# Attention score bursts of 9 and 10 banks, and P tiles that take the place expected to be free first

## The chip, the cores and the metric

One core of a Trainium2 chip. The metric is device time in microseconds (us). TensorE (PE; its weight loads are PEld), VectorE (DVE), ScalarE (ACT), GpSimd (POOL) and SyncE (SP) each run their own instructions in order and wait for one another by semaphores; DMAs are issued from the queues of SP, ACT and POOL.

## The reference, cut to what matters

The output is a mix of two branches over the same input of 2048 tokens by 1024. The change touches only the attention branch: 32 heads of 32 columns each.

```python
qkv = (x @ wqkv).reshape(B, S, 3, H, Dh).transpose(2, 0, 3, 1, 4)
q, k, v = qkv[0], qkv[1], qkv[2]
scores = jnp.einsum("bhqd,bhkd->bhqk", q, k) * (Dh ** -0.5)
p = _softmax(scores, axis=-1)
o = jnp.einsum("bhqk,bhkd->bhqd", p, v)
a = o.transpose(0, 2, 1, 3).reshape(B, S, D) @ wo
...
return g * a + (1 - g) * b
```

S is 2048, H is 32, Dh is 32; everything is float32. The other branch (b, a choice among 64 experts) and the gate g are worked out ahead of the attention's heads and behind them.

## The kernel before, in words

The program runs in three stages. From the start to about 628 us it makes q, k and v, the expert branch and the sums for the last products. From there to about 1650 us it works off the 32 heads, one behind the other: this is the stage of the change. Behind it come the products with wo and the output.

A head has 16 key tiles of 128 keys (kt, 0 to 15). For one tile, TensorE makes scores of 128 keys against 2048 queries: four matmuls of 512 queries, each into one of the banks of a ring of 7 PSUM banks (L1305, tile `ring`). Each matmul has a weight load of its own. ScalarE takes 1 to 4 neighbouring banks of the ring at a time, and writes exp of them into a P tile of 128 by 2048 in SBUF (L1319). A bank may be written again once its exp has ended. TensorE then multiplies P with V, 32 columns for each of four quarters of the queries side by side (L1330), and sums over the 16 tiles in one PSUM bank, `o`; behind the last tile ScalarE copies it out (`finish`, L1429, tile `osb`).

The row sums of P are made beside this: VectorE adds the tiles of a head into `acc`, two instructions a tile (L1366). Three tiles of each head (kt 3, 8 and 12, the rest of the list SUMS at L1340) are added by a DMA from POOL's queue into `accd` instead (L1354), and kt 1 is written straight into `accd`. When a head is over, VectorE adds `acc` and `accd` (merge), and further DMAs and adds fold the sums of up to four heads into one tile, of which `head_sums` makes the row sums by a matmul (L1345) into one bank of the ring.

A P tile lives in one of 11 places in SBUF (P0 to P7, and the tiles named vhl, wo_raw2 and wo_raw3, which serve for weights near the end). In the last third there are 9 and then 8 places. `p_tile` hands them out in rotation. A place can be written again when P·V and the add, or the DMA, that read its old tile have ended; ScalarE waits for that ahead of a tile's first exp.

The order of the work is written out by the loop at L1550 to L1565. It counts half tiles: `ends` gives where each burst of scores ends, 4 half tiles (8 banks) or 5 (10 banks), seven bursts a head, of 8, 8, 8, 10, 10, 10 and 10 banks. A half tile is 256 of each 512 queries, so that two banks make one half of a tile; two of a head's bursts end in the middle of a tile. Behind each burst stands P·V up to four half tiles behind the last score, then what `todo` has for these tiles (finish, merges, folds, loads for the next head on SP's queue), and the tile's add (`presum`). `scores` (L1282) sets by `cuts` where one exp ends and the next begins: at the burst's end, at a tile's end, at the ring's end, and behind the first bank, or the first three in a burst of 10.

Of the kernel before, what the change touches and what calls it, by code (L numbers as in the profile page):

```python
# [13 lines left out]
AF = mybir.ActivationFunctionType  # L14
# [5 lines left out]
H = 32  # L20
KC = D // 128
HC = KC // 2
NT = S // 128
NQ = S // 512
G = H // 4
W = 256
SCALE = 32 ** -0.5
# [5 lines left out]
def gated_mha_peer_kernel(ctx, tc, xT, wqkv, wv, wo, wq, k12, ug, v, out):  # L33
# [8 lines left out]
    nc = tc.nc  # L42
# [301 lines left out]
    places = {(2, 0): "xh2", (2, 1): "xl1", (3, 0): "xh3", (3, 1): "xl2"}  # L344
# [361 lines left out]
    for blk, (k, n) in enumerate(order):  # L706
        w, c = chunks[k]
        t = pairs[k % 2]
# [441 lines left out]
    P, pools, keep = {}, {}, None  # L1150


    RING = (11, 0), (9, 28 * 11), (8, 28 * 11 + 12 * 9)
    LATE = 21, 28

    def p_tile(h, kt):


        k, (n, i) = pools["next"], RING[0]
        for places, i0 in RING[1:]:  # L1160
            if k >= i0:
                n, i = places, i0
        i = (k - i) % n
        pools["next"] += 1
        pool, name = ((pools["right"], f"P{i}") if i < 4 else (pools["left"], f"P{i}") if i < 8 else
                      (keep, ("vhl", "wo_raw2", "wo_raw3")[i - 8]))
        P[h, kt] = pool.tile([128, S], F32, name=name)
        return P[h, kt]

    def first_scores():  # L1170

        tp.close()
        pools.update(right=Pool("ppr", side="right"), next=0)
        K, Q = Z
        pt = p_tile(0, 0)
        for qc, i in enumerate((5, 6, 0, 1)):
            ps = ps1.tile([128, 512], F32, name=f"bk{i}")
            c = slice(qc * 512, (qc + 1) * 512)
            nc.tensor.matmul(ps, K[:98, :128], Q[:98, c], start=True, stop=True)
            nc.scalar.activation(pt[:, c], ps, AF.Exp, scale=SCALE)  # L1180
# [48 lines left out]
    NB = 7  # L1229
    ring = pss.tile([128, NB, 512], F32, name="ring")  # L1230
# [30 lines left out]
    nc.vector.memset(KQ[1][0][96:98, :].bitcast(F32), 1.0)  # L1261
    load_head(1)

    def by_half(t):

        return t.rearrange("p (q f m) -> p q f m", q=NQ, f=2)

    def parts_of(u0, u1):

        while u0 < u1:  # L1270
            (h, u), whole = divmod(u0, 2 * NT), u0 % 2 == 0 and u0 + 1 < u1
            yield h, u // 2, None if whole else u % 2
            u0 += 2 if whole else 1

    def columns(t, part, i, m=1):

        f = part[2]
        if f is None:
            return t[:, i * 512:(i + m) * 512].rearrange("p (a m) -> p a m", a=m)
        return by_half(t)[:, 2 * i:2 * (i + m), f, :]  # L1280

    def scores(u0, u1):  # L1282


        of = [(part, i) for part in parts_of(u0, u1) for i in range(NQ if part[2] is None else 2)]
        n = len(of)
        banks = ring_banks(n)
        ends = {c for c in range(1, n + 1) if c == n or of[c][1] == 0 or banks[c] == 0}
        if n > 2 * NQ:
            cuts = ends | {1, 2, 3}  # L1290
        else:
            cuts = ends | {1}
            cuts |= {c + 2 for c in range(NQ, n, NQ) if not cuts & {c + 1, c + 3}}
        c0 = 0
        for c, i in enumerate(banks):
            part, j = of[c]
            h, kt, f = part
            K, Q = KQ[h % 2]
            if f is None:
                q = Q[:98, j * 512:(j + 1) * 512]  # L1300
                s = ring[:, i, :]
            else:
                q = by_half(Q)[:98, 2 * j:2 * j + 2, f, :]
                s = ring[:, i, :].rearrange("p (a m) -> p a m", a=2)
            on_ring(nc.tensor.matmul(s, K[:98, kt * 128:(kt + 1) * 128], q, start=True, stop=True), i)  # L1305
            if c + 1 not in cuts:
                continue
            m = c + 1 - c0
            j -= m - 1
            if j == 0 and f != 1:  # L1310
                if kt == SUMS[h == H - 1][0]:
                    P[h, kt] = ACCD[h] = wk.tile([128, S], F32, name="accd")
                else:
                    p_tile(h, kt)
            i -= m - 1
            s = ring[:, i:i + m, :]
            if f is not None:
                s = s.rearrange("p a (b m) -> p (a b) m", b=2)
            on_ring(nc.scalar.activation(columns(P[h, kt], part, j, m), s, AF.Exp, scale=SCALE),  # L1319
                    *range(i, i + m))  # L1320
            c0 = c + 1

    def pv(h, kt, f):
        g, j = divmod(h, 4)
        p = P[h, kt]
        if kt == 0 and f != 1:
            O[h] = pso.tile([128, 512], F32, name="o")
        c0, c1 = (0, 512) if f is None else (256 * f, 256 * f + 256)
        for qc in range(NQ):
            nc.tensor.matmul(O[h][32 * qc:32 * qc + 32, c0:c1], Vt[g][:, kt, 32 * j:32 * j + 32],  # L1330
                             p[:, qc * 512 + c0:qc * 512 + c1], start=(kt == 0), stop=(kt == NT - 1))
# [4 lines left out]

    SUMS = (1, 3, 8, 12), (2, 4, 6)  # L1340

    def rowsum(ps, *srcs, ones=ones):
        for src in srcs:
# [5 lines left out]
    def presum(h, kt):  # L1349
        sums = SUMS[h == H - 1]  # L1350
        if kt == 0 or kt == sums[0] or (h == H - 1 and kt >= NT - 2):
            return
        if kt in sums:
            nc.gpsimd.dma_start(ACCD[h], P[h, kt], accum_op=OP.add)  # L1354
            return
        if kt == 1 + (sums[0] == 1):
            if h > 0:
                ACC[h] = wk.tile([128, S], F32, name="acc")
            add(ACC[h], P[h, 0], P[h, kt])
        else:  # L1360
            add(ACC[h], ACC[h], P[h, kt])
# [185 lines left out]
    at((H - 1) * NT + 2, load_rb, 0, 0, KC - 1, range(2, 4))  # L1547


    LAG, LAST = 4, 2 * NT * H  # L1550
    ends = [6] + [2 * NT * h + e for h in range(H - 1) for e in (8, 12, 16, 21, 26, 31, 36)]
    ends += [*range(ends[-1] + 4, LAST + 1, 4), LAST + LAG]
    u0, v0, k = 2, 0, 0
    for u1 in ends:
        scores(u0, min(u1, LAST))
        v1 = 2 if u1 == 6 else u1 - LAG
        for part in parts_of(v0, v1):
            pv(*part)
        while 2 * k + 2 <= u1:
            for f, a in todo.pop(k, []):  # L1560
                f(*a)
            if k < NT * H:
                presum(*divmod(k, NT))
            k += 1
        u0, v0 = u1, v1  # L1565
    assert not todo
    pss.close()
    pools["left"].close()
# [281 lines left out]
```

## Time and profile before

| | us |
|---|---|
| three runs: median (lowest, highest) | 1819.63 (1819.18, 1826.15) |
| the execution that was profiled: its own time | 1828.57 |
| its span, from the first to the last instruction | 1826.8 |
| PE busy in it | 1813.0 |
| DVE busy | 1499.7 |
| ACT busy | 1229.4 |
| exps into the places named P (L1319, 917 instructions) | 735.9 |

The profile shows one execution. A line of the order in time has the start, the time from the start of the first to the end of the last of the instructions that it merges, the engine, the line of the program, the operation, out and in, and a count; in brackets is how long the engine had been idle ahead of it and who ended that. PE counts as busy while a matmul is in its pipeline, so waits on TensorE are seen better in the distances between its weight loads. Windows give the busy time of each engine in a stretch, and behind them the granted clock of TensorE, the mean busy share of the 16 DMA engines and GB/s.

### The profile page before, as it was taken

How to read it: one execution, taken by the hardware profiler on the slowest of the kernel's cores; microseconds unless marked ns; L12 is line 12 of the kernel's file. 1: busy time of each engine (PE TensorE's matmuls, PEld its weight loads, DVE VectorE, ACT ScalarE, POOL GpSimd, SP SyncE). 2: the span in 40 equal slices, each digit the busy share in tenths (PEclk: the TensorE clock that was granted, in tenths of full speed). 3: DMA queues.
4: the chain of work that ended last, by engine and by line, in shares of the span. 5: the costliest groups of instructions: out<-in, count | busy, mean ns of one | idle time of the engine just before them, and what ended most of it. 6: DMA issues, size and time to landing. Idle time of an engine off the chain costs nothing.

```text
span 1826.8 us, 27633 instructions
## 1 busy us (share of the span) xinstructions
PE 1813.0 (99%) x10383; PEld 1130.7 (62%) x10383; DVE 1499.7 (82%) x1673; ACT 1229.4 (67%) x1618; POOL 261.5 (14%) x314
## 2 busy tenths in 40 slices
PE   9999999999999999999999999999999999999999
PEld 7777777788888744445444444454444444447887
DVE  7868785368987788998989999898999898996674
ACT  4434422211243499999999999999899999993221
POOL 0222000036301211111111111111111011101000
PEclk9999999999999999999999999999999999999999
DMA  6788888722248689999999999999999998976861
GB/s 234 238 281 257 266 264 308 254 65 98 81 150 288 220 187 198 193 184 200 179 200 197 196 212 196 191 195 205 186 194 204 190 205 185 199 171 206 278 171 58
DMA packets 132224, 364.72 MB, mean 200 GB/s; under 512 B 17540, under 2 KB 57876, under 8 KB 106168
## 3 DMA queue, kind: packets, MB, share of 16 engines
q0 software_dynamic: 22064, 136.07, 37.8%
q1 hardware_dynamic: 89864, 190.94, 35.0%
q10 hardware_dynamic: 20160, 35.92, 7.0%
q8 instruction: 82, 1.34, 0.3%
q14 instruction: 54, 0.44, 0.1%
HBM read 169.14 MB, written 72.10 MB: 132 GB/s over the span
## 4 chain that ended last, share of the span: by engine, by line
PE 87%; DMA 10%; ACT 1%; DVE 1%; issue 0%; POOL 0%; SPq 0%; ACTq 0%; DVEq 0%; POOLq 0%
PE ring L1305 23%; PE o L1330 21%; PE bk L157 12%; PE bk L713 10%; DMA accd<-P 6%; PE pa L157 6%; PE bk L760 5%; PE pa L1594 2%; PE bk L928 2%; DMA accd<-wo_raw 2%; PE bk L313 2%; PE bk L493 1%; PE pa L1601 1%; PE bk L397 1%; DMA wraw<-in_wqkv 1%; ACT P L1319 1%
## 5 line engine op out<-in xcount | busy, mean ns | idle before, releaser
L1319 ACT ACTIVATE P<-ring 128x512 f32<-128x512 f32 (+3 forms) x917 | 735.9, 903 | 19.7 <-DMA accd<-P 5.2
L1366 DVE TENSOR_TENSOR acc<-acc,P 128x1024 f32<-128x1024 f32 x512 | 586.9, 1216 | 5.8 <-ACT P L1319 5.5
L1330 PE MATMUL o<-P,V 128*32 128x512 f32 (+1 forms) x3464 | 373.1, 551 | 0.0
L1305 PE MATMUL ring<-Q,K 98*128 98x512 f32 x1024 | 275.9, 410 | 3.2 <-ACT P L1319 2.2
L1305 PE MATMUL ring<-z,z 98*128 98x512 f32 x1020 | 275.9, 411 | 2.0 <-ACT P L1319 1.9
L1305 PEld LDWEIGHTS ring<-Q,K 98*128 98x128 f32 x1024 | 183.5, 188 | 133.8 <-ACT P L1319 44.4
L1305 PEld LDWEIGHTS ring<-z,z 98*128 98x128 f32 x1020 | 182.7, 188 | 132.0 <-ACT P L1319 43.8
L1330 PEld LDWEIGHTS o<-P,V 128*32 128x32 f32 x3464 | 94.7, 109 | 185.5 <-issue 167.8
L1354 POOL DMA_DIRECT2D accd<-P x76 | 69.2, 910 | 469.4 <-ACT P L1319 277.2
L1366 DVE TENSOR_TENSOR rb<-acc,accd 32x1024 f32<-32x1024 f32 (+2 forms) x60 | 70.7, 1217 | 52.1 <-DMA accd<-P 38.9
L1319 ACT ACTIVATE wo_raw<-ring 128x512 f32<-128x512 f32 (+2 forms) x135 | 110.1, 899 | 3.3 <-DMA accd<-wo_raw 1.5
L242 ACT ACTIVATE hi<-bk 128x512 fp32r<-128x512 f32 x40 | 23.7, 595 | 112.4 <-PE bk L713 93.2
L713 PE MATMUL bk<-xh,e 128*128 128x512 f32 x384 | 94.2, 394 | 0.0
L713 PE MATMUL bk<-xl,e 128*128 128x512 f32 x384 | 92.2, 389 | 0.0
L1366 DVE TENSOR_TENSOR acc<-acc,wo_raw 128x1024 f32<-128x1024 f32 x74 | 86.0, 1216 | 0.1
L713 PEld LDWEIGHTS bk<-xh,e 128*128 128x128 f32 x384 | 71.0, 188 | 22.0 <-issue 3.4
L713 PEld LDWEIGHTS bk<-xl,e 128*128 128x128 f32 x384 | 72.1, 188 | 15.0
L1319 ACT ACTIVATE vhl<-ring 128x512 f32<-128x512 f32 (+3 forms) x97 | 80.7, 900 | 0.9 <-PE ring L1305 0.2
L255 DVE TENSOR_TENSOR lo<-bk,hi 128x512 fp32r<-128x512 f32 x40 | 27.6, 689 | 65.1 <-ACT hi L242 62.7
L103 DVE TENSOR_TENSOR e<-wraw,e 128x512 fp32r<-128x512 f32 (+3 forms) x64 | 54.9, 867 | 29.7 <-ACT e L102 28.9
L102 ACT ACTIVATE e<-wraw 128x512 fp32r<-128x512 f32 (+3 forms) x64 | 44.7, 705 | 41.5 <-DMA wraw<-in_wqkv 26.1
L157 PE MATMUL bk<-xh,e 128*128 128x512 f32 x288 | 68.7, 393 | 0.0
(305 smaller groups left out, 2539.4 us busy)
## 6 DMA issues: line engine op xcount, KB each, us to landing
accd<-P POOLq DMA_DIRECT2D x76, 1024.0 KB, 11.6
wqt<-in_wq SPq DMA_DIRECT2D x26, 1024.0 KB
wraw<-in_wqkv SPq DMA_DIRECT2D x30, 512.0 KB
accd<-wo_raw POOLq DMA_DIRECT2D x11, 1024.0 KB, 12.5
rb<-acc POOLq DMA_DIRECT2D x36, 256.0 KB, 7.7
qdh<-hi ACTq DMA_DIRECT2D x32, 256.0 KB
qdl<-lo ACTq DMA_DIRECT2D x32, 256.0 KB
kdh<-hi ACTq DMA_DIRECT2D x32, 256.0 KB
```

The costliest lines, as they stand in the source:

```text
L102: nc.scalar.activation(hi, src, AF.Copy)
L103: (on or nc.vector).tensor_tensor(out=lo, in0=src, in1=hi.bitcast(F32), op=OP.subtract)
L157: nc.tensor.matmul(ps, self.a[a][i][:, k, :], self.b[b][j][k], start=(not first and k == 0 and i == j == 0), stop=(k == HC - 1 and i == 1))
L313: nc.tensor.matmul(ps[32 * quad:32 * quad + 32, :], kpad[:, quad % 2, i, :], t[:, quad, :], start=(i == 0), stop=(i == 3))
L713: nc.tensor.matmul(ps, t[:, kc // HC, a, kc % HC], x_at(b, n, kc), start=first, stop=last)
L760: nc.tensor.matmul(ps, x_at(a, t // 4, kc)[:, tok], b, start=first, stop=last)
L928: nc.tensor.matmul(p, x_at(a, t // 4, kc)[:, tok], b, start=first, stop=last)
L1305: on_ring(nc.tensor.matmul(s, K[:98, kt * 128:(kt + 1) * 128], q, start=True, stop=True), i)
L1319: on_ring(nc.scalar.activation(columns(P[h, kt], part, j, m), s, AF.Exp, scale=SCALE), *range(i, i + m))
L1330: nc.tensor.matmul(O[h][32 * qc:32 * qc + 32, c0:c1], Vt[g][:, kt, 32 * j:32 * j + 32], p[:, qc * 512 + c0:qc * 512 + c1], start=(kt == 0) ...
L1354: nc.gpsimd.dma_start(ACCD[h], P[h, kt], accum_op=OP.add)
L1366: nc.vector.tensor_add(out[:, c], a[:, c], b[:, c])
```

## The change

The loop counts banks, not half tiles. A head's bursts have 9, 9, 9, 10, 9, 9 and 9 banks (in the order in which they lie from a head's start: the first of them, up to the end at 73, ends 9 banks into the next head), and may end behind any bank of a tile. Scores of a bank are always of 512 neighbouring queries; the half tiles of 256 remain for P·V alone, which follows 8 banks behind, rounded down to a half tile. The first exps of one bank are now one in a burst of 8, two in a burst of 9, three in a burst of 10. In the last head the bursts have 8 banks as before.

`p_tile` keeps for each place the tile number at which it is expected to be free (`until`): 14 tiles on for a tile that a DMA adds, 4 for any other. It takes the place with the smallest number.

```diff
-        k, (n, i) = pools["next"], RING[0]
-        for places, i0 in RING[1:]:
-            if k >= i0:
-                n, i = places, i0
-        i = (k - i) % n
+        n = [places for places, k in PLACES if pools["next"] >= k][-1]
         pools["next"] += 1
+        i = min(range(n), key=lambda i: until[i])
+        until[i] = h * NT + kt + (14 if kt in SUMS[h == H - 1] else 4)
...
-        of = [(part, i) for part in parts_of(u0, u1) for i in range(NQ if part[2] is None else 2)]
-        n = len(of)
+        n = s1 - s0
         banks = ring_banks(n)
-        ends = {c for c in range(1, n + 1) if c == n or of[c][1] == 0 or banks[c] == 0}
-        if n > 2 * NQ:
-            cuts = ends | {1, 2, 3}
-        else:
-            cuts = ends | {1}
+        cuts = {c for c in range(1, n + 1) if c == n or (s0 + c) % NQ == 0 or banks[c] == 0}
+        cuts |= set(range(1, max(1, n - NB) + 1))
+        if n <= 2 * NQ:
             cuts |= {c + 2 for c in range(NQ, n, NQ) if not cuts & {c + 1, c + 3}}
...
-    LAG, LAST = 4, 2 * NT * H
-    ends = [6] + [2 * NT * h + e for h in range(H - 1) for e in (8, 12, 16, 21, 26, 31, 36)]
-    ends += [*range(ends[-1] + 4, LAST + 1, 4), LAST + LAG]
+    LAG, HEAD = 2 * NQ, NQ * NT
+    ends = [3 * NQ] + [HEAD * h + e for h in range(H - 1) for e in (18, 27, 36, 46, 55, 64, 73)]
+    ends[-1] -= 1
+    ends += [*range(ends[-1] + LAG, HEAD * H + 1, LAG), HEAD * H + LAG]
...
-        v1 = 2 if u1 == 6 else u1 - LAG
+        v1 = 2 if s1 == 3 * NQ else (s1 - LAG) // 2
```

On TensorE, at the turn from head 0 to head 1 (Q_5228 and K_5227 are head 1's, z_ are head 0's; a P·V row of 32x512 is a whole tile, one of 32x256 a half), the order before is:

```order
L1305 MATMUL ring<-z_4627,z_4626 128x512 x10
L1330 MATMUL o<-wo_raw_5371,V 32x512 x4
L1330 MATMUL o<-P_5382,V 32x512 x4
L1330 MATMUL o<-P_5402,V 32x256 x4
L1305 MATMUL ring<-z_4627,z_4626 128x512 x2
L1305 MATMUL ring<-Q_5228,K_5227 128x512 x8
L1330 MATMUL o<-P_5402,V 32x256 x4
L1330 MATMUL o<-P_5414,V 32x512 x4
L1330 MATMUL o<-P_5418,V 32x512 x4
L1305 MATMUL ring<-Q_5228,K_5227 128x512 x8
```

and after the change, at the same place:

```order
L1284 MATMUL ring<-z_4627,z_4626 128x512 x9
L1308 MATMUL o<-vhl,V 32x256 x4
L1308 MATMUL o<-wo_raw_5363,V 32x512 x4
L1308 MATMUL o<-wo_raw_5367,V 32x256 x4
L1284 MATMUL ring<-z_4627,z_4626 128x512 x9
L1308 MATMUL o<-wo_raw_5367,V 32x256 x4
L1308 MATMUL o<-P_5393,V 32x512 x4
L1308 MATMUL o<-P_5396,V 32x512 x4
L1284 MATMUL ring<-Q_5228,K_5227 128x512 x9
L1308 MATMUL o<-P_5419,V 32x512 x4
L1308 MATMUL o<-P_5429,V 32x512 x4
L1284 MATMUL ring<-Q_5228,K_5227 128x512 x9
```

A burst of 10 that ran across the turn, and P·V of two and a half tiles behind it, have become a burst of 9 that begins with the new head, and P·V of two tiles; a burst of 9 follows where one of 8 did.

On ScalarE, from the end of head 0 on (the digits behind P are the places; `waits` names what a place's old readers or the scores are waited for: DVE, a DMA of POOL's queue as DMASW, PE), the order before is:

```order
L1319 ACTIVATE accd_5452<-ring_5229 128x2048 [waits PE_49]
L1429 ACTIVATE osb_5475<-o_5257 128x512 [waits PE_49]
L1319 ACTIVATE P5_5479<-ring_5229 128x512 [waits DVE_49,PE_49]
L1319 ACTIVATE P5_5479<-ring_5229 128x512 [waits PE_49]
L1319 ACTIVATE P5_5479<-ring_5229 128x1024 [waits PE_49]
L1319 ACTIVATE P6_5488<-ring_5229 128x1024 [waits DVE_49,PE_49]
L1319 ACTIVATE P6_5488<-ring_5229 128x1024 [waits PE_49]
L1319 ACTIVATE P7_5509<-ring_5229 128x512 [waits DMASW4_49,PE_49]
```

and after the change:

```order
L1296 ACTIVATE accd_5469<-ring_5229 128x2048 [waits PE_49]
L1296 ACTIVATE P6_5472<-ring_5229 128x512 [waits DVE_49,PE_49]
L1405 ACTIVATE osb_5482<-o_5257 128x512 [waits PE_49]
L1296 ACTIVATE P6_5472<-ring_5229 128x512 [waits PE_49] x3
L1296 ACTIVATE vhl_5495<-ring_5229 128x2048 [waits DVE_49,PE_49]
L1296 ACTIVATE wo_raw2_5498<-ring_5229 128x512 [waits DVE_49,PE_49]
L1296 ACTIVATE wo_raw2_5498<-ring_5229 128x512 [waits PE_49] x3
```

The copy `osb` stood behind the last exp of the burst that crosses the turn, and ahead of a burst of 8; it stands now one bank into the tile kt 2, ahead of a burst of 9. Place P7, which a DMA of kt 8 reads, was taken again eleven tiles on; now the places go on past it, and it is left until later.

More of the change, by code (lines that the diff above doesn't have):

```diff
@@ L1150, in gated_mha_peer_kernel @@
     P, pools, keep = {}, {}, None
-    RING = (11, 0), (9, 28 * 11), (8, 28 * 11 + 12 * 9)
+    SUMS = (1, 3, 8, 12), (2, 4, 6)
+    PLACES = (11, 0), (9, 28 * 11), (8, 28 * 11 + 12 * 9)
     LATE = 21, 28
+    until = [0] * PLACES[0][0]
     def p_tile(h, kt):
-        k, (n, i) = pools["next"], RING[0]
-        for places, i0 in RING[1:]:
-            if k >= i0:
-                n, i = places, i0
-        i = (k - i) % n
+        n = [places for places, k in PLACES if pools["next"] >= k][-1]
         pools["next"] += 1
+        i = min(range(n), key=lambda i: until[i])
+        until[i] = h * NT + kt + (14 if kt in SUMS[h == H - 1] else 4)
         pool, name = ((pools["right"], f"P{i}") if i < 4 else (pools["left"], f"P{i}") if i < 8 else
@@ L1262, in gated_mha_peer_kernel @@
     load_head(1)
-    def by_half(t):
-        return t.rearrange("p (q f m) -> p q f m", q=NQ, f=2)
     def parts_of(u0, u1):
@@ L1273, in parts_of, with scores @@
             u0 += 2 if whole else 1
[L1275 to L1282, printed above, removed]
-        of = [(part, i) for part in parts_of(u0, u1) for i in range(NQ if part[2] is None else 2)]
-        n = len(of)
-        banks = ring_banks(n)
-        ends = {c for c in range(1, n + 1) if c == n or of[c][1] == 0 or banks[c] == 0}
-        if n > 2 * NQ:
-            cuts = ends | {1, 2, 3}
-        else:
-            cuts = ends | {1}
+    def scores(s0, s1):
+        n = s1 - s0
+        banks = ring_banks(n)
+        cuts = {c for c in range(1, n + 1) if c == n or (s0 + c) % NQ == 0 or banks[c] == 0}
+        cuts |= set(range(1, max(1, n - NB) + 1))
+        if n <= 2 * NQ:
             cuts |= {c + 2 for c in range(NQ, n, NQ) if not cuts & {c + 1, c + 3}}
@@ L1295, in scores @@
         for c, i in enumerate(banks):
-            part, j = of[c]
-            h, kt, f = part
+            (h, kt), qc = divmod((s0 + c) // NQ, NT), (s0 + c) % NQ
             K, Q = KQ[h % 2]
[L1299 to L1305, printed above, removed]
+            on_ring(nc.tensor.matmul(ring[:, i, :], K[:98, kt * 128:(kt + 1) * 128],
+                                     Q[:98, qc * 512:(qc + 1) * 512], start=True, stop=True), i)
             if c + 1 not in cuts:
@@ L1308, in scores @@
             m = c + 1 - c0
-            j -= m - 1
-            if j == 0 and f != 1:
+            q0 = qc + 1 - m
+            if q0 == 0:
                 if kt == SUMS[h == H - 1][0]:
@@ L1315, in scores @@
             i -= m - 1
[L1316 to L1320, printed above, removed]
+            on_ring(nc.scalar.activation(
+                P[h, kt][:, q0 * 512:(q0 + m) * 512].rearrange("p (a m) -> p a m", a=m),
+                ring[:, i:i + m, :], AF.Exp, scale=SCALE), *range(i, i + m))
             c0 = c + 1
@@ L1331, in pv @@
                              p[:, qc * 512 + c0:qc * 512 + c1], start=(kt == 0), stop=(kt == NT - 1))
-    SUMS = (1, 3, 8, 12), (2, 4, 6)
     def rowsum(ps, *srcs, ones=ones):
@@ L1547, in gated_mha_peer_kernel @@
     at((H - 1) * NT + 2, load_rb, 0, 0, KC - 1, range(2, 4))
-    LAG, LAST = 4, 2 * NT * H
-    ends = [6] + [2 * NT * h + e for h in range(H - 1) for e in (8, 12, 16, 21, 26, 31, 36)]
-    ends += [*range(ends[-1] + 4, LAST + 1, 4), LAST + LAG]
-    u0, v0, k = 2, 0, 0
-    for u1 in ends:
-        scores(u0, min(u1, LAST))
-        v1 = 2 if u1 == 6 else u1 - LAG
+    LAG, HEAD = 2 * NQ, NQ * NT
+    ends = [3 * NQ] + [HEAD * h + e for h in range(H - 1) for e in (18, 27, 36, 46, 55, 64, 73)]
+    ends[-1] -= 1
+    ends += [*range(ends[-1] + LAG, HEAD * H + 1, LAG), HEAD * H + LAG]
+    s0, v0, k = NQ, 0, 0
+    for s1 in ends:
+        scores(s0, min(s1, HEAD * H))
+        v1 = 2 if s1 == 3 * NQ else (s1 - LAG) // 2
         for part in parts_of(v0, v1):
             pv(*part)
-        while 2 * k + 2 <= u1:
+        while NQ * (k + 1) <= s1:
             for f, a in todo.pop(k, []):
@@ L1564, in gated_mha_peer_kernel @@
             k += 1
-        u0, v0 = u1, v1
+        s0, v0 = s1, v1
     assert not todo
```

## The prediction

> **What bounds the kernel now.** I read the page's busy line and chain first, to find the stage; then the table of windows over the attention stage; then the order in time of the weight loads (PEld, the sharpest clock of what TensorE does, since each stands at its own start), beside ScalarE's exps.
>
> ```profile
> PE 1813.0 (99%) x10383; PEld 1130.7 (62%) x10383; DVE 1499.7 (82%) x1673; ACT 1229.4 (67%) x1618; POOL 261.5 (14%) x314
> PE ring L1305 23%; PE o L1330 21%; PE bk L157 12%; PE bk L713 10%; DMA accd<-P 6%; PE pa L157 6%; PE bk L760 5%; PE pa L1594 2%; PE bk L928 2%; DMA accd<-wo_raw 2%; PE bk L313 2%; PE bk L493 1%; PE pa L1601 1%; PE bk L397 1%; DMA wraw<-in_wqkv 1%; ACT P L1319 1%
> ```
>
> Scores (L1305) and P·V (L1330) hold the longest shares of the chain, and a DMA that adds a P tile into accd holds 8% more. So I look at the stage in which they run.
>
> ```profile
> 800.00:900.00 100.00, 99.74 (x662) 49.12 (x661) 85.16 (x77) 97.72 (x126) 14.75 (x19) 1.00 0.91 188
> 900.00:1000.00 100.00, 98.31 (x660) 47.31 (x658) 90.66 (x82) 95.67 (x119) 15.52 (x19) 1.00 0.95 195
> 1000.00:1100.00 100.00, 98.35 (x644) 48.27 (x641) 93.62 (x84) 94.63 (x121) 15.05 (x18) 0.98 0.96 202
> 1100.00:1200.00 100.00, 100.00 (x670) 49.33 (x668) 90.48 (x81) 98.12 (x124) 15.21 (x18) 1.00 0.94 190
> 1300.00:1400.00 100.00, 97.76 (x642) 47.75 (x635) 92.52 (x83) 94.31 (x122) 14.63 (x18) 0.98 0.93 197
> ```
>
> The columns are length, PE, PEld, DVE, ACT, POOL, granted clock, DMA share. Four resources stand above 90% at once, so whichever is relieved hands over to the next at little distance. In most stretches PE has no gap; in three it loses 1.7 to 2.2 us, twice with a lower clock.
>
> ```profile
> 1107.97 1.69 PEld L1305 LDWEIGHTS ring<-Q,K 98*128 98x128 f32 x8 [0.84 <-ACT accd L1319]
> 1110.02 0.16 PEld L1330 LDWEIGHTS o<-P,V 128*32 128x32 f32 x8 [0.36 <-PE ring L1305]
> ...
> 1111.87 1.68 PEld L1305 LDWEIGHTS ring<-Q,K 98*128 98x128 f32 x8 [0.84 <-ACT P L1319]
> ...
> 1119.68 1.91 PEld L1305 LDWEIGHTS ring<-Q,K 98*128 98x128 f32 x9 [0.84 <-ACT P L1319]
> 1121.85 0.19 PEld L1305 LDWEIGHTS ring<-Q,K 98*128 98x128 f32 x1 [0.25 <-ACT P L1319]
> 1122.27 0.16 PEld L1330 LDWEIGHTS o<-wo_raw,V 128*32 128x32 f32 x8 [0.24 <-issue]
> ...
> 1124.56 0.53 PEld L1305 LDWEIGHTS ring<-Q,K 98*128 98x128 f32 x3 [0.41 <-issue]
> ```
>
> This is one head's rhythm. A burst of 8 banks takes 1110.02 - 1107.97 = 2.05 us and P·V of two tiles 1.85 (1111.87 - 1110.02). A burst of 10 takes 1122.27 - 1119.68 = 2.59, P·V of two and a half tiles 2.29. A head is 3 x (2.05 + 1.85) + 4 x (2.59 + 2.29) = 31.2 us. The bracket 0.84 in front of a burst is no stall: it is TensorE working through the last P·V passes. The stall is in the ten-bank burst: nine weight loads follow each other, the tenth comes late because its ring bank still waits for the burst's third exp. How much that costs: eight loads make a row of 1.69 us and nine one of 1.91, so a bank more costs 0.22 to 0.23, and ten banks without a stall would take 2.05 + 2 x 0.23 = 2.51. **The ring's stall is 0.08 us a burst, 0.32 us a head**, far less than the brackets suggest.
>
> **The change part by part.** First, the stalls of whole microseconds, which the new choice of places addresses.
>
> ```profile
> 1021.46 1.45 PEld L1305 LDWEIGHTS ring<-z,z 98*128 98x128 f32 x7 [0.84 <-ACT wo_raw L1319]
> 1024.99 0.19 PEld L1305 LDWEIGHTS ring<-z,z 98*128 98x128 f32 x1 [2.08 <-ACT P L1319]
> ```
> ```profile
> 1018.08 3.99 ACT L1319 ACTIVATE wo_raw<-ring 128x512 f32<-128x512 f32 x4
> 1024.35 1.08 ACT L1319 ACTIVATE P<-ring 128x512 f32<-128x512 f32 x2 [2.27 <-DMA accd<-P]
> ```
> ```profile
> 1011.79 0.90 POOL L1354 DMA_DIRECT2D accd<-P  x1 [6.32 <-DMA accd<-P]
> ```
>
> TensorE waits for ScalarE, and ScalarE waits for the place of a P tile that the DMA issued at 1011.79 still reads; it lands 12.5 us later. With rotation a tile's place comes again after 11 or 12 tiles, 23 us at 31.2/16 = 1.95 us a tile. The new rule holds a DMA's source 14 tiles and any other 4, plus a common slack x: with 12 others and 3 sources a head in 11 places, 12(4 + x) + 3(14 + x) = 11 x 16 gives x = 5.7. Sources then rest 19 to 20 tiles, 38 us, and the others 9 to 10, 18 to 19 us. So these waits go. Their price in the profiled execution, by the windows: 0.26 + 1.69 + 1.65 + 2.24 = 5.8 us of missing PE time, and twice 2% of 100 us at the lower clock, 4.0 us; 9.8 us together. The execution with the profile took 1828.57 us (span 1826.8 and 1.8 around it); the median of the three runs, 1819.63, is 8.9 below. I take the difference to be these waits, which leaves about 0.9 us of them in an ordinary run. **Term: -0.9 us on the median, -9.8 on the profiled execution.**
>
> At the clock a rule can be weighed. The Trainium skill's page "TensorE: Matmul & The Clock Gate" (Practical rules on idle gaps) holds that a gap of more than about 3 us returns the array to half rate until about 3.4 us of work have passed. The two windows at 0.98 agree in size (half of 3.4 us is 1.7, the windows give 2.0), though the gap between weight loads that set it off here was 2.1 us.
>
> Second, the bursts. Per head six of 9 and one of 10, with P·V of 5, 4, 5, 5, 4, 5, 4 half tiles: four of 2.29 and three of 1.85 as before, so P·V terms cancel (two more tiles are split per head; the split ones already stand inside the 2.29). A nine-bank burst without stall is 2.05 + 0.23 = 2.28. It reuses two banks of its own, not three, so it needs the second exp only. Is that in time?
>
> ```profile
> 1125.09 2.93 ACT L1319 ACTIVATE P<-ring 128x512 f32<-128x512 f32 x4
> ```
> ```profile
> 1125.59 1.08 ACT L1319 ACTIVATE P<-ring 128x512 f32<-128x512 f32 x2
> ```
> ```profile
> 1131.89 1.91 ACT L1319 ACTIVATE P<-ring 128x2048 f32<-128x2048 f32 x1
> 1133.65 1.80 ACT L1319 ACTIVATE vhl<-ring 128x1024 f32<-128x1024 f32 x2
> ```
> ```profile
> L1319 ACT ACTIVATE P<-ring 128x512 f32<-128x512 f32 x521 | 283.5, 609 | 16.7 <-DMA accd<-P 5.2 <-PE ring L1305 4.5
> ```
>
> The first exp starts 1125.09 - 1124.56 = 0.53 after the burst. Two single-bank exps take 1.08, one 0.61, so they follow each other by 0.47; a four-bank one is followed after 1.76, so a further bank costs 0.43. The second exp of a nine-bank burst ends at 0.53 + 1.1 = 1.63; the ninth weight load is due at 1.91 - 0.19 = 1.72. In time, by 0.09. So six bursts at 2.28 and one at 2.59 against 4 x 2.59 + 3 x 2.05: 16.27 against 16.51, **-0.24 us a head**.
>
> But ScalarE needs 5 x 0.47 + 4 x 0.43 = 4.1 us for nine banks in five exps, and a nine-bank burst with P·V of two tiles lasts 2.28 + 1.85 = 4.13. Where two and a half tiles follow it has 0.4 us over; where two follow it has nothing. The head's last P·V is now one of two tiles, and behind it ScalarE also copies the head's output (osb).
>
> ```profile
> 1108.22 0.65 ACT L1429 ACTIVATE osb<-o 128x512 f32<-128x512 f32 x1
> 1108.70 3.84 ACT L1319 ACTIVATE P<-ring 128x512 f32<-128x512 f32 x4
> ```
>
> Before, this copy ran 0.25 us into an eight-bank burst (1108.22 - 1107.97) and held its exps for 0.48, up to 0.73; eight banks reuse one bank, and nothing waited. After, ScalarE ends its exps at 0.53 + 4.1 - 4.13 = 0.50 into the next burst, copies until 0.98, and the second exp ends at 0.98 + 1.1 = 2.08. The ninth weight load stands at about 2.13 instead of 1.72. A late last load is followed by P·V after 0.42 (1122.27 - 1121.85), a timely one after 0.55, so the burst ends at 2.55, not 2.28: +0.27 a head. What is queued behind the copy is the next burst's exps, and TensorE behind them; the P·V of 2.29 that follows lets ScalarE catch up. **Sum of the bursts: -0.24 + 0.27, about 0, x 31 heads = +1 us at most.** Bounds: if the copy slips in without a wait, -0.24 x 31 = -7.4, and without the ten-bank stall too -10; if the copied burst's exps run in six pieces and wait for their banks, 0.2 more, +6.
>
> The head_sums turns (10 of them) put one bank and one copy into the ring as before; a copy that ends at 0.73 leaves the second exp at 1.83, 0.1 late, at most 1 us in all. 32 exps fewer (1194 to 1162) are on ScalarE, not on the path. DMAs, VectorE's adds and SP's loads are the same in number and order; loads of the next head's K and Q go out at a head's last tile and have a whole head.
>
> From the profiled execution: 1828.6 - 9.8 + 0 = 1818.8; from the median: 1819.6 - 0.9 + 0 = 1818.7. I forecast **1818.5 us, no change that can be told**.
>
> One rule speaks against the row. The Trainium skill's page "ScalarE: Activation LUTs" (What ACT_TABLE_LOAD costs) gives 186 ns plus 0.833 ns per element, with an overlap of about 93 ns between neighbours, so 0.52 us from one single-bank exp to the next, where this trace shows 0.47. By it nine banks would need 4.3 us and the late ninth load would be 0.2 us later at each head, some 6 us in sum, 1825. The measured row decides.
>
> **The rivals.**
>
> A, faster: the copy's wait does not arise, or is covered by the 0.13 us that a late last load gives back and by ScalarE starting early. For it: 0.09 us of reserve in each nine-bank burst and ScalarE's 0.4 us over behind each longer P·V. Against it: the addition above has to be wrong by 0.4 us. It gives 1818.5 - 7.4 to - 10, about 1810.
>
> B, slower: VectorE becomes the one that frees the places late. Places that it empties now return after 9 to 10 tiles, not 11 to 12; with 9 and 8 places, in the last twelve heads, after 7 to 8 and 6 to 7.
>
> ```profile
> 1024.36 2.36 DVE L1366 TENSOR_TENSOR rb<-acc,accd 32x1024 f32<-32x1024 f32 x2 [4.20 <-DMA accd<-P]
> ...
> 1033.57 4.62 DVE L1366 TENSOR_TENSOR acc<-acc,wo_raw 128x1024 f32<-128x1024 f32 x4
> ```
>
> VectorE stood 4.2 us for the same late DMA, and then read the two tiles that ScalarE had written from 1018.08 and about 1020.1 until 1038.2: 18 us for the second. Nine tiles are 9 x 1.95 = 17.6. That is the point from which it decides: here it would cost 0.5 us, and since ScalarE no longer loses time at the DMA, VectorE's lag is not made up there either. At worst all 9.8 us of the profiled waits come back in this form in every run: 1828 to 1829. Against it: this is the profile's latest tile, and an ordinary run has a tenth of those waits.
>
> C, slower by less: ScalarE is late behind every short P·V, not only behind the copy. It has 0.03 us there. If each exp cost 0.05 more, it would come 0.2 late at the copy alone, since elsewhere 0.09 of reserve and 0.13 at the end of a burst cover it: +6 us, 1825.
>
> That the change does not do what it says (the DMA's waits stay) gives 1819 to 1820, inside the forecast.
>
> **How the numbers follow.** Forecast 0.55, rival A 0.21, B 0.13, C 0.11. The forecast's own range is 1813 to 1823. To leave no more than 2 in 10 out, the whole range takes in A's middle and most of B: 1807 to 1828. A difference of 0.5% is 9.1 us (about what a measurement tells from no change): under 1810.5 lies most of A, 0.18; over 1828.7 the worst of B and C together, 0.10; between, 0.72.
>
> **What the changed profile would show.** Nine-bank bursts of 2.28 us nearly everywhere; the one behind the copy 2.5 to 2.6, its last weight load in a row of its own with ScalarE as the releaser. A head of 31.2 us without head_sums. No wait of ScalarE for a DMA accd<-P. ScalarE waits, where it has any for a place, released by VectorE. I am wrong if a head lasts 30.9 or less (A), if it lasts 31.4 or more (C), or if gaps of microseconds stay with VectorE's adds in front (B).

## The result, and the profile after

| us | before | after |
|---|---|---|
| median of 14 runs each on one chip (lowest, highest) | 1820.93 (1816.68, 1826.15) | 1820.57 (1820.15, 1827.73) |
| 12 runs of after and 17 of before on a second chip | 1817.91 (1815.82, 1825.21) | 1820.44 (1819.31, 1820.95) |
| the profiled execution (its span) | 1828.57 (1826.8) | 1820.81 (1819.0) |

The ratio is 1.0003, with an interval of 0.9992 to 1.0015; on the second chip (run e8, below) 1.0009, 0.9998 to 1.0019. There is no change that can be told, as forecast. But the table holds two changes of opposite sign: the lowest run became 3.5 us longer on both chips, and the median came from 4.2 and 2.1 us above the lowest run to 0.4 and 1.1 above it. On the first chip they cancel; on the second the median is 2.5 us higher after the change.

The busy line and the chain of the page of after:

```profile
PE 1811.4 (100%) x10879; PEld 1147.2 (63%) x10879; DVE 1499.6 (82%) x1673; ACT 1225.7 (67%) x1586; POOL 261.4 (14%) x314
PE 98%; DMA 1%; ACT 1%; SPq 0%; issue 0%; DVE 0%; ACTq 0%; DVEq 0%
```

The 8% that DMAs into accd held of the chain are gone. What ScalarE waited for between 620 and 1650 us (us in total, times, the longest): first, of before, its waits for a DMA alone; then, of after, the longest waits of the heads:

```profile
ACT P L1319 <- DMA accd<-P: 5.2, 2, 2.9
ACT wo_raw L1319 <- DMA accd<-wo_raw: 1.5, 1, 1.5
```
```profile
ACT P L1296 <- PE ring L1284: 10.0, 44, 0.3
ACT ssb L1412 <- PE ring L1321: 4.3, 9, 0.6
ACT wo_raw L1296 <- PE ring L1284: 1.7, 7, 0.3
```

After the change an exp waits for scores alone: no DMA and no add of VectorE's stands ahead of it (the row with ssb is the copy of the row sums, which waits for head_sums). The windows of after, at the places where before lost PE time and clock (length, PE, PEld, DVE, ACT, POOL, clock, DMA share):

```profile
900.00:1000.00 100.00, 100.00 (x718) 51.16 (x718) 95.43 (x86) 97.43 (x124) 15.04 (x18) 1.00 0.96 204
1000.00:1100.00 100.00, 100.00 (x717) 50.83 (x717) 91.83 (x83) 97.22 (x120) 15.14 (x18) 1.00 0.92 196
1300.00:1400.00 100.00, 100.00 (x725) 50.48 (x717) 91.36 (x82) 97.79 (x118) 14.31 (x17) 1.00 0.96 206
```

PE is never idle, and the clock stays at 1.00. Yet the span is only 7.8 us shorter than that of an execution that had lost 9.8 by its windows. The rest is in the weight loads at the turn from one head to the next:

```profile
1098.25 1.92 PEld L1284 LDWEIGHTS ring<-Q,K 98*128 98x128 f32 x9 [0.84 <-issue]
1100.53 0.16 PEld L1308 LDWEIGHTS o<-P,V 128*32 128x32 f32 x8 [0.36 <-issue]
...
1102.38 1.45 PEld L1284 LDWEIGHTS ring<-Q,K 98*128 98x128 f32 x7 [0.84 <-ACT accd L1296]
1104.14 0.19 PEld L1284 LDWEIGHTS ring<-Q,K 98*128 98x128 f32 x1 [0.31 <-ACT P L1296]
1104.63 0.19 PEld L1284 LDWEIGHTS ring<-Q,K 98*128 98x128 f32 x1 [0.30 <-ACT P L1296]
1105.05 0.16 PEld L1308 LDWEIGHTS o<-wo_raw,V 128*32 128x32 f32 x8 [0.24 <-issue]
...
1129.60 1.92 PEld L1284 LDWEIGHTS ring<-z,z 98*128 98x128 f32 x9 [0.84 <-ACT P L1296]
...
1133.73 1.45 PEld L1284 LDWEIGHTS ring<-z,z 98*128 98x128 f32 x7 [0.84 <-ACT accd L1296]
```

The burst ahead of the turn is timely: 1100.53 - 1098.25 = 2.28 us. The one behind it lasts 1105.05 - 1102.38 = 2.67, and here both its eighth and its ninth load stand in rows of their own. From turn to turn it is 1133.73 - 1102.38 = 31.35 us, against 31.21 before. ScalarE at the same place:

```profile
1102.46 0.65 ACT L1296 ACTIVATE P<-ring 128x512 f32<-128x512 f32 x1
1102.94 0.66 ACT L1405 ACTIVATE osb<-o 128x512 f32<-128x512 f32 x1
1103.41 7.38 ACT L1296 ACTIVATE P<-ring 128x512 f32<-128x512 f32 x10
```

The exp at 1102.46 is the last of the burst before (one bank of kt 2). The copy starts 0.56 into the new burst, the new burst's first exp 1.03 into it, where 0.53 is usual.

### The profile page after: what moved, and what is told of

Same layout as the page of the kernel before. It is cut to its first block, busy times and chain, and to the rows that moved or that the text cites. A ratio compares the mean times of both kernels' runs of the same rounds, so it can differ in the third digit from the quotient of the medians.

```text
span 1819.0 us, 28606 instructions
## 1 busy us (share of the span) xinstructions
PE 1811.4 (100%) x10879; PEld 1147.2 (63%) x10879; DVE 1499.6 (82%) x1673; ACT 1225.7 (67%) x1586; POOL 261.4 (14%) x314
## 4 chain that ended last, share of the span: by engine, by line
PE 98%; DMA 1%; ACT 1%; SPq 0%; issue 0%; DVE 0%; ACTq 0%; DVEq 0%
PE ring L1284 29%; PE o L1308 25%; PE bk L157 13%; PE bk L713 10%; PE pa L157 6%; PE bk L760 5%; PE pa L1571 2%; PE bk L928 2%; PE bk L313 2%; PE bk L493 1%; PE pa L1578 1%; PE bk L397 1%; DMA wraw<-in_wqkv 1%; PE ring L1321 0%; ACT P L1296 0%; DMA V<-od 0%
## 5 line engine op out<-in xcount | busy, mean ns | idle before, releaser
L1308 PE MATMUL o<-P,V 128*32 128x512 f32 (+1 forms) x3864 | 377.8, 507 | 0.0
L1308 PEld LDWEIGHTS o<-P,V 128*32 128x32 f32 x3864 | 108.3, 109 | 198.3 <-issue 180.3
L1296 ACT ACTIVATE wo_raw<-ring 128x512 f32<-128x512 f32 (+3 forms) x137 | 113.3, 900 | 2.8 <-PE ring L1284 1.7
L1296 ACT ACTIVATE vhl<-ring 128x512 f32<-128x512 f32 (+3 forms) x97 | 84.9, 946 | 1.3 <-PE ring L1284 0.9
L1342 DVE TENSOR_TENSOR acc<-acc,wo_raw 128x1024 f32<-128x1024 f32 x68 | 79.8, 1217 | 0.3 <-ACT wo_raw L1296 0.3
L1342 DVE TENSOR_TENSOR acc<-acc,vhl 128x1024 f32<-128x1024 f32 x62 | 72.9, 1217 | 0.3 <-ACT vhl L1296 0.3
## 6 DMA issues: line engine op xcount, KB each, us to landing
accd<-wo_raw POOLq DMA_DIRECT2D x9, 1024.0 KB, 10.6
```

The costliest lines, as they stand in the source:

```text
L1296: on_ring(nc.scalar.activation(P[h, kt][:, q0 * 512:(q0 + m) * 512].rearrange("p (a m) -> p a m", a=m), ring[:, i:i + m, :], AF.Exp, scale ...
L1342: nc.vector.tensor_add(out[:, c], a[:, c], b[:, c])
```

## The experiments

The theory: undoing the rotation saves waits of whole microseconds that only some executions have, and the copy at the turn costs 0.13 us a head, 4 us, in every execution. The rivals: the bursts cost nothing and the places bring nothing (the waits only move elsewhere); or the cost is one of the nine-bank bursts in general, not of the copy. Later a further one was added, S: that TensorE's waits at head_sums for the chain of folds hide what is won.

**e1_places_only**: before, with the new choice of places alone.

```diff
-        i = (k - i) % n
...
+        i = min(range(n), key=lambda i: until[i])
+        until[i] = h * NT + kt + (14 if kt in SUMS[h == H - 1] else 4)
```

> The kernel before with the new choice of places alone; bursts of 8 and 10 banks stay. Theory T (two terms that cancel: the places save the DMA waits, some 4 us in a median run, and the bursts give them back, 0.13 us a head): a head stays at 31.2 us, ScalarE no longer waits for a DMA accd<-P, and the time is 1816 to 1817.5 with little spread, about 4 us under the kernel before. Rival N (neither part does anything on the chip): 1821, with the spread of before. Rival V (VectorE's adds take over the waits): ScalarE waits for places behind VectorE's adds, 1819 or more.

Measured: 1817.42 us (1815.83 to 1821.05, 12 runs) against 1817.96 of before on that chip (1815.56 to 1827.94, 35 runs); ratio 0.9992, 0.9982 to 1.0002. No run is longer than 1821.05, where 10 of the 35 of before are, and no exp waits for a DMA; but the median gained 0.5, not 4 (by the ratio 1.5). Its profiled run was the longest, and shows a stall of another kind, in PEld's order in time and in the window around it:

```profile
914.78 0.13 PEld L1330 LDWEIGHTS o<-accd,V 128*32 128x32 f32 x4 [0.30 <-issue]
917.58 0.19 PEld L1344 LDWEIGHTS ring<-rb,ones 128*32 128x32 f32 x8 [2.67 <-issue]
918.61 2.81 PEld L1305 LDWEIGHTS ring<-Q,K 98*128 98x128 f32 x8 [0.84 <-issue]
```
```profile
900.00:1000.00 100.00, 98.20 (x656) 47.84 (x648) 93.19 (x84) 94.73 (x118) 15.07 (x18) 0.98 0.95 197
```

TensorE stands 2.67 us at head_sums (L1344), and the eight loads behind it take 2.81 instead of 1.69: lower clock again. That head lasts 35.6 instead of 32.1. The wait is for the last DMA of the folds: POOL issued it at 907.1, and it landed 10.2 us later, at 917.3. So head_sums has waits of its own, which places don't touch. The profiled execution of before had one too, in PEld's order:

```profile
917.35 0.19 PEld L1345 LDWEIGHTS ring<-rb,ones 128*32 128x32 f32 x8 [1.66 <-ACT P L1319]
```

The releaser that the row names is not the one: the usual gap here is 0.30, and the folds' last DMA, issued at 907.64, landed 9.4 us later, at 917.0.

**e2_bursts_only**: after, with the old rotation of places.

```diff
-        i = min(range(n), key=lambda i: until[i])
-        until[i] = h * NT + kt + (14 if kt in SUMS[h == H - 1] else 4)
...
+        i = (k - i) % n
```

> The changed kernel with the old rotation of places. Theory T: a head of 31.35 us where nothing waits, and the DMA waits of before come on top, so 1823 to 1826, 3 to 5 us over the kernel before, with a spread of several us. Rival N: 1821. A second rival, that the bursts alone save time and the places lose it: under 1819.

Measured: 1822.30 us (1820.47 to 1826.93); ratio 1.0022, 1.0010 to 1.0033. The bursts alone cost 4 us in the median and 4.9 in the lowest run. Heads last 31.3 to 31.4, as in after. The profiled run had a single wait for a DMA:

```profile
ACT P L1297 <- DMA accd<-P: 0.4, 1, 0.4
```

So its 1820.96 us are almost the bursts' cost by itself. That the bursts cost nothing is out.

**e3_late_copy**: after, with the copy `osb` put off until the second exp of the next burst has been issued.

```diff
+            exps += 1
+            if exps == 2:
+                while copies:
+                    finish(copies.pop(0))
...
-            at(base + NT, finish, h)
+            at(base + NT, copies.append, h)
```

> The changed kernel, with the copy of a head's output put behind the first two exps of the next burst on ScalarE instead of ahead of them. Theory T (the copy ahead of a nine-bank burst costs 0.40 us a head): the burst behind a head's end falls from 2.68 to 2.28 us, a head to 30.95, and the time to about 1808 to 1809. Rival R (the long burst comes from the ring or from the head's new K and Q, not from the copy): the burst stays at 2.6 to 2.7 and the time at 1820 to 1821.

Measured: 1811.74 us (1810.27 to 1819.95); ratio 0.9962, 0.9945 to 0.9979. PEld and ACT at a turn:

```profile
1104.70 1.94 PEld L1286 LDWEIGHTS ring<-Q,K 98*128 98x128 f32 x9 [0.84 <-ACT accd L1298]
1106.98 0.16 PEld L1314 LDWEIGHTS o<-wo_raw,V 128*32 128x32 f32 x8 [0.34 <-ACT osb L1411]
...
1109.27 1.69 PEld L1286 LDWEIGHTS ring<-Q,K 98*128 98x128 f32 x8 [0.41 <-issue]
1111.16 0.19 PEld L1286 LDWEIGHTS ring<-Q,K 98*128 98x128 f32 x1 [0.21 <-ACT P L1298]
1111.60 0.37 PEld L1314 LDWEIGHTS o<-P,V 128*32 128x32 f32 x12 [0.25 <-issue]
```
```profile
1104.78 1.62 ACT L1298 ACTIVATE P<-ring 128x512 f32<-128x512 f32 x3
1106.21 0.68 ACT L1411 ACTIVATE osb<-o 128x512 f32<-128x512 f32 x1
```

The burst behind the turn is back at 2.28 (1106.98 - 1104.70), the one behind that at 2.33. Heads without head_sums last 30.95 to 31.08, 0.35 less than in after, for one copy that has moved by two exps. This shows the copy as the cost at the turn, not the nine-bank bursts in general. The runs fall into two groups: eight from 1810.3 to 1811.8, one of 1814.6, and three from 1818.7 to 1820.0. The profiled run (1818.68) is of the longer kind, and shows where: PEld, and POOL's DMAs ahead of it:

```profile
1039.41 0.13 PEld L1314 LDWEIGHTS o<-wo_raw,V 128*32 128x32 f32 x4 [0.30 <-issue]
1043.67 0.23 PEld L1327 LDWEIGHTS ring<-rb,ones 128*32 128x32 f32 x8 [4.13 <-DVE acc L1348]
1045.56 2.64 PEld L1286 LDWEIGHTS ring<-Q,K 98*128 98x128 f32 x7 [1.66 <-issue]
```
```profile
1023.89 1.37 POOL L1336 DMA_DIRECT2D accd<-P  x1
1033.05 0.78 POOL L1399 DMA_DIRECT2D rb<-acc  x1 [7.80 <-issue]
```

head_sums (L1327) stands 4.1 us. The row names an add of VectorE's, but it was the fold's last DMA: POOL issued it at 1033.05, after 7.8 us of idle time in which the fold ahead of it was under way (it landed at 1031.2), and it took 10.6 us to land, at 1043.6. The load at 1043.67 follows. Then seven loads take 2.64 us instead of 1.45.

**e4_eight_behind**: after, with the burst that runs behind a head's end cut to 8 banks, and the next made 10.

```diff
-    ends = [3 * NQ] + [HEAD * h + e for h in range(H - 1) for e in (18, 27, 36, 46, 55, 64, 73)]
+    ends = [3 * NQ] + [HEAD * h + e for h in range(H - 1) for e in (17, 27, 36, 46, 55, 64, 73)]
```

> The changed kernel with the first burst behind a head's end cut to 8 banks and the one behind it made 10 (8, 10, 9, 10, 9, 9, 9). Theory T: eight banks reuse one ring bank only and so the copy hides there (2.05 us, no long last loads), the second burst of ten costs its 0.08 us; a head of 31.0 us and a time of about 1811. Rival R (the turn of the head is slow whatever burst follows): a burst of 2.3 or more there, 1820 or more.

Measured: 1821.56 us (1821.00 to 1822.60); ratio 1.0014, 1.0004 to 1.0025. A miss of T, by 10 us; R's time came, but not its burst of 2.3 or more. PEld at the turn:

```profile
1102.47 1.45 PEld L1284 LDWEIGHTS ring<-Q,K 98*128 98x128 f32 x7 [0.84 <-ACT accd L1296]
1104.23 0.19 PEld L1284 LDWEIGHTS ring<-Q,K 98*128 98x128 f32 x1 [0.31 <-ACT P L1296]
1104.66 0.16 PEld L1308 LDWEIGHTS o<-wo_raw,V 128*32 128x32 f32 x8 [0.25 <-PE ring L1284]
...
1106.52 1.69 PEld L1284 LDWEIGHTS ring<-Q,K 98*128 98x128 f32 x8 [0.84 <-ACT P L1296]
1108.45 0.19 PEld L1284 LDWEIGHTS ring<-Q,K 98*128 98x128 f32 x1 [0.25 <-ACT P L1296]
1108.94 0.19 PEld L1284 LDWEIGHTS ring<-Q,K 98*128 98x128 f32 x1 [0.30 <-ACT P L1296]
1109.37 0.16 PEld L1308 LDWEIGHTS o<-P,V 128*32 128x32 f32 x8 [0.25 <-issue]
```

The burst of 8 lasts 2.19, not 2.05, and the burst of 10 behind it 2.85, not 2.59 (over 30 heads 2.12 to 2.21 and 2.71 to 2.86). The short burst leaves ScalarE less time (2.19 + 1.86 us for eight banks), so the copy's lag is still there when the next burst starts, and that one reuses three banks. The lag is paid one burst later. That is read from these rows; no run takes it apart further.

**e5_late_both** and **e6_places_late_sums**: the late copy, and the places alone, with head_sums and what follows it moved six tiles back.

```diff
-                at(base + NT + 18, head_sums, h - 3, 4)
-            at(base + NT + (22 if g < FOURS else 14), load_r, g)
-            at(base + NT + (30 if g < FOURS else 18), norm_r, g)
+                at(base + NT + 24, head_sums, h - 3, 4)
+            at(base + NT + (28 if g < FOURS else 14), load_r, g)
+            at(base + NT + (34 if g < FOURS else 18), norm_r, g)
```

> The kernel with the late copy, and with the row-sum matmul of four heads (head_sums) six tiles later, its load and norm after it. Theory S (what is left of waits is TensorE standing at head_sums for the last DMA of the fold chain; it shows once per some runs as 5 us and a clock drop): heads of 31.0 us, no wait at head_sums, time 1808 to 1810 with a spread of 2 us or less. Rival V (VectorE's adds hold the places, so that a later head_sums only moves the wait): ScalarE waits behind VectorE, time and spread like the late copy alone, 1811 to 1812 with runs up to 1820.

> The kernel before with the new places and the later head_sums, bursts of 8 and 10. Theory S: both waits are gone, 1815.5 to 1816.5 with a spread of 2 us or less: this is the pace of the old bursts alone, 31.22 us a head. Rival V: as with the places alone, 1817.4 with runs up to 1821 or more.

Both change a part of the computation: the next group's first merge, at 19 tiles, now comes ahead of head_sums and overwrites the tile T from which the row sums of four heads are made; these sums are other ones. It also makes TensorE wait for that merge and its folds. Measured: 1861.97 us (ratio 1.0242, 1.0223 to 1.0260) and 1850.78 (1.0182, 1.0161 to 1.0202). They tell nothing of S; the shift had to be smaller.

**e7_hold24**: after, with a DMA's source held for 24 tiles, not 14, so that the other places come back sooner: a test of VectorE as the one that frees them late.

```diff
-        until[i] = h * NT + kt + (14 if kt in SUMS[h == H - 1] else 4)
+        until[i] = h * NT + kt + (24 if kt in SUMS[h == H - 1] else 4)
```

> The changed kernel with 24 tiles instead of 14 expected for a tile that a DMA reads: the other tiles' places then return after about 8 tiles (15 us) in the first two thirds, 6 to 7 and 4 to 5 in the last. It measures how much room VectorE has. Theory T (VectorE frees a place 9 to 18 us after its tile is begun): ScalarE waits for places behind VectorE, some us in the first heads and more in the last, time 1825 to 1845. Rival (VectorE is far ahead, no room is used): 1820 to 1821, as with 14.

Measured: 1827.95 us (1825.05 to 1832.27, 6 runs); ratio 1.0055, 1.0035 to 1.0075, and 7.5 over after on the same chip. Now ScalarE does wait for VectorE:

```profile
ACT P L1296 <- DVE acc L1342: 2.0, 6, 0.6
```

All six are in heads 28 and 29, with 8 places; in the first heads, where T expected some too, there are none. So the edge exists, and the change stands on the near side of it. The waits don't make up 7.5. The profiled run is 6.1 over that of after on the same chip (e8): 1.4 in head 28, and 4.7 behind the attention stage, where TensorE waits 2.8 us for ScalarE's `z`, and VectorE 5.9 instead of 1.8 for the last row sums to come back by DMA. Why these are late is open.

**e8_after_again**: after, unchanged, beside e5 to e7 on their chip.

> The changed kernel as it is, beside the others on one chip. All theories: 1820 to 1821, heads of 31.35 us, no wait of ScalarE for a DMA. It gives the base for the other three, and with the kernel before it tells whether the ratio of 1.000 holds on another chip: by the two terms it would be 1.001 to 1.002 where the kernel before has few DMA waits.

Measured: 1820.44 us (1819.31 to 1820.95); ratio 1.0009, 0.9998 to 1.0019, in the table above. Its profiled run has heads of 31.28 to 31.41 (without head_sums), and no wait of ScalarE for a DMA.

**e9_copy_sums20** and **e10_places_sums20**: the late copy, and the places alone, with head_sums two tiles later and two steps of the chain of folds shifted to fit.

```diff
-                at(base + NT + 3, merge4, h)
-                at(base + NT + 5, fold4, h)
+                at(base + NT + (3 if j else 5), merge4, h)
+                at(base + NT + (5 if j else 6), fold4, h)
...
-                at(base + NT + 18, head_sums, h - 3, 4)
+                at(base + NT + 20, head_sums, h - 3, 4)
```

> The kernel with the late copy, with head_sums of four heads two tiles later, and, to make room, the first merge of the next group of four two tiles later and its fold one. Theory S (the runs of the late copy that lie 3 to 10 us above its lowest stand at head_sums for the fold chain): heads of 31.0 us, median within 1 us of the late copy's lowest run, 1810 to 1811, and hardly a run over 1813. Rival V (the waits lie elsewhere or only move): median and spread of the late copy, 1811 to 1812 with runs to 1820.

> The kernel before with the new places and the same shift of head_sums. Theory S: median 1816 to 1816.5, spread 2 us. Rival V: as the places alone, 1817.4 with a spread of 5 us.

Both still change a part: behind heads 20 to 23 comes the first pair, whose merge stays at 19 tiles, so the sums of these four heads are other ones, and head_sums there has to wait for that merge. Measured: e9 1811.40 us (1810.65 to 1819.44), ratio 0.9960, 0.9945 to 0.9975; e10 1822.75 (1817.61 to 1827.28), ratio 1.0003, 0.9987 to 1.0018, where S expected about 1816. In e10's profile the only stall is at the changed place; in PEld's order:

```profile
1424.91 0.17 PEld L1344 LDWEIGHTS ring<-rb,ones 128*32 128x32 f32 x4 [3.91 <-issue]
1427.88 2.03 PEld L1305 LDWEIGHTS ring<-Q,K 98*128 98x128 f32 x8 [1.66 <-issue]
```

At that place e9's profiled run, its lowest, has none. So e10 cannot be held against S, nor for it.

**e12_late_copy_again**: the late copy of e3, beside e9 on the same chip.

> The late copy once more, beside the one with the later head_sums. All theories: 1811 to 1812, some runs several us above. It is the base for that one.

Measured: 1819.04 us (1811.72 to 1822.53); ratio 0.9986, 0.9971 to 1.0001. The profiled run, its lowest, has heads of 31.0 and no stall at head_sums; in the last head, whose bursts have 8 banks, one P·V waits 1.5 us for the copy (as in e11, below). With head_sums two tiles later (e9) nine of 12 runs lie under 1812.6, without (e12) three. That speaks for S in the late copy, and the landings in e1, e3 and before show that head_sums does stand for the folds' last DMA; but the two intervals touch, and the sums of four heads differ, so it is not shown that this makes up the long runs.

**e11_before_late_copy**: before, with the same late copy as e3.

> The kernel before, with its head's copy behind the first two exps of the next burst, as in the late copy. Theory T (behind a head of before stands an eight-bank burst, which waits for one exp only, so the copy costs nothing there): no change, ratio 0.999 to 1.001. Rival (the copy costs 0.3 to 0.4 us a head in any order): 8 to 12 us less.

Measured: 1846.56 us (1846.14 to 1846.84, 4 runs); ratio 1.0141, 1.0118 to 1.0164. A miss: it is no edit without effect. PEld and ACT behind a turn:

```profile
951.01 1.68 PEld L1307 LDWEIGHTS ring<-z,z 98*128 98x128 f32 x8 [0.84 <-ACT accd L1321]
954.23 0.16 PEld L1336 LDWEIGHTS o<-P,V 128*32 128x32 f32 x8 [1.54 <-ACT osb L1435]
```
```profile
951.55 2.15 ACT L1321 ACTIVATE vhl<-ring 128x512 f32<-128x512 f32 x2
953.59 0.59 ACT L1435 ACTIVATE osb<-o 128x512 f32<-128x512 f32 x1
```

In a burst of 8 the second exp has three banks, so the copy starts 2.58 us into the burst and ends at 3.17. The next head's P·V, due at 2.05, needs the bank `o` that the copy reads, and starts at 3.22. That is 1.17 us in most heads, and heads of 32.4 instead of 31.2. In e3 the second exp has one bank, the copy ended 2.19 into the burst, and P·V stood at 2.28. In e11 P·V followed 0.05 behind the copy's end, so e3 had some 0.04 us to spare.

## Why the prediction was right, and which terms cancelled

- **Nine banks without a stall: right.** Forecast 2.28, measured 2.28 (median of 184; 144 of the 180 between 640 and 1590 us stand within 2.25 to 2.30). The ten-bank burst and P·V stayed at 2.59, 2.29 and 1.85. Where the copy hides (e3), heads of 31.0 against 31.22 in e1 give 0.2 us for the nine-bank bursts, near the working's 0.24.
- **The copy at the turn: the mechanism right, the size too small.** Forecast 0.27 us more, a burst of 2.55; measured 2.67, so 0.39 more. The working took the copy to end at 0.98 and the ninth load to stand at 2.13. The exp behind the copy started at 1.03, 0.05 later; it and the next lasted 1.16 together, not 1.1; and the ninth load stood at 1104.63 - 1102.38 = 2.25, 0.12 later than forecast. That is the whole of it. Over 30 turns the burst lasts 2.61 to 2.69. The step "-0.24 + 0.27, about 0" is the term mis-sized: it is -0.24 + 0.39 = +0.15, of which the turn-to-turn time shows 0.14. Over 31 heads that is +4 us, not "+1 us at most"; the lowest runs say 3.5 (after) and 4.9 (e2).
- **The places: right that the waits go, too small what an ordinary run has of them.** All waits for a DMA's place went (after, e1, e8). I took 0.9 us of them for an ordinary run, from three runs. With 14, 17 and 29 to 35 runs, the median of before is 2.1 to 4.4 us above its lowest on every chip, and that of after 0.4 and 1.1. So the change took some 1 to 4 us off that distance. The places alone (e1) took 0.5 off the median, by the ratio 1.5 (its interval reaches from 3.3 off to 0.4 more), and left it 1.6 above the lowest run; the bursts alone (e2) left it 1.8 above, before 2.4 on that chip. Slower heads also give the folds more time ahead of head_sums; no run separates that from the places. In the profiled execution, from the first weight load of the scores to the end of their last burst, the stage lasted 1015.5 us in before, 1008.0 in after and 1007.9 in e1, which without its 3.5 us stall is 1004.4: before had lost 11.1 there, not 9.8, and the bursts cost 3.5. Nor was all of that loss waits for places, as the working has it: 1.4 us of it was the wait at head_sums at 917.35. How the spread over all runs of before divides between the two is not settled.
- **So the number was right in part by luck, through two errors of opposite sign**: 3.5 to 4 us too little for the bursts, and up to 3 too little for the waits that the change as a whole took out of an ordinary run. The forecast was 1.1 us under the median shown; the medians of 14 runs lie 0.4 apart, and 1820.57, 2.1 over the forecast, stands within its own range. On the second chip, where before had less to lose, the same change left the median 2.5 us higher.
- **Rival A** (the copy slips in, heads of 30.9): not in after, but e3 makes it so by moving the copy, at 1810.3 in its lowest run, as A's price said (about 1810).
- **Rival B** (VectorE frees the places late): not in after. e7 shows that it begins where sources are held 24 tiles.
- **Rival C** (every short P·V late): its size, 31.4 a head, nearly came (heads without head_sums last 31.28 to 31.56, about 31.35 as a rule); its mechanism did not, since the bursts behind the other short P·Vs are timely.
- **The exps.** From 1102.46 to 1102.94 and 1103.41, ScalarE's single-bank instructions follow by 0.48 and 0.47 us, as in before. The Trainium skill's page "ScalarE: Activation LUTs" (What ACT_TABLE_LOAD costs), whose figures make it 0.52 by estimate and so made 1825, is not borne out here.

The late copy (e3, e12) is the version that beat the kernel before clear of noise on one chip: 0.9962, where after stands at 1.0003 and 1.0009 in its two sets of runs. On another chip it stands at 0.9986, 0.9971 to 1.0001, which can't be told from no change. Its lowest runs are 5.3 and 4.9 us under those of before; what its other runs lose is the open question of S.

## What to carry to other kernels

Before pricing a stall that one profile shows, look at the spread of many runs: the distance of the median from the lowest run bounds what such waits cost an ordinary run, as far as the lowest is free of them. Where an engine has next to no time over in a cycle, a small operation in its queue is priced by what stands behind it until the lag is made up; making the next step shorter (e4) only moves the lag on. And the right place for a copy lies between two deadlines, the banks that the exps must free and the bank that the copy itself must free: with a small exp ahead of it there was just room for it (e3, some 0.04 us), with a large one there was none (e11, 1.2 us a head).

## What the runs showed of the hardware

TensorE's rate dropped after gaps as short as 2.1 us between weight loads (before, ahead of the load at 1024.99: the granted clock was 0.50 from 1026 to 1028.9), but not after 1.66 (before, 917.35: 1.00 from 917 to 925). Behind 2.67 us in e1, eight loads took 2.81 us instead of 1.69, at a clock of 0.50 from 919 to 922; behind 4.13 in e3, seven took 2.64 instead of 1.45, at 0.50 from 1043 to 1049. So a wait of 2.7 us cost 3.5 in the head's length. The Trainium skill's page "TensorE: Matmul & The Clock Gate" (Why this matters for your kernels) sets the limit at gaps of more than about 3 us; before and e1 went under it, e3 agrees. That section holds the rule that the prediction cites under another heading.

A last weight load that comes late does not shift all that follows by its lateness: P·V started 0.42 us behind a late one and 0.55 behind a timely one, so up to 0.13 us of lateness cost nothing there.
